# Six pairs of rounds convolved by VectorE instead of four, with each task's first product on ScalarE

## The chip, the core and the metric

The kernel runs on one core of one Trainium2 chip. The core has five engines, each with its own instruction queue: TensorE (PE in the profile, with its weight loads as PEld), VectorE (DVE), ScalarE (ACT), GpSimd (POOL) and SyncE (SP). An engine works through its queue in order, so an instruction that waits holds up everything behind it. Data move between DRAM and the on-chip memory SBUF by DMAs, which are issued from SP and POOL and share 16 DMA engines. TensorE writes to PSUM, from which ScalarE and VectorE take the results.

The metric is the time of one execution in microseconds (us). Less is better.

## What is computed

A causal convolution over seven tokens, whose taps are softmaxed per head of 24 channels, and then a feed-forward part without a bias (cut from the reference):

```
w = exp(weight - max); w = w / (sum(w) + 1e-09)           # 8 heads x 7 taps
x_pad = concatenate([zeros(B, 6, D), x], axis=1)          # B=8, S=3904, D=192
out[b, s, h*24+g] = sum_k w[h, k] * x_pad[b, s + k, h*24+g]
a = conv @ w1                                             # 31232 x 192 @ 192 x 1024
b = conv @ w2
h = a * b @ w3                                            # w3: 1024 x 1024
return h @ w_out                                          # w_out: 1024 x 192
```

The kernel multiplies w3 by w_out once, at the start (`w3_product`, into `W_sb`), so that each token costs two products with 1024 columns and one product back to 192.

## The kernel before

**Rounds.** The 31232 tokens are two streams of 15616 (NS = 2), worked side by side in the upper and lower 64 partitions. A round is 512 tokens of both streams (CH = 512); there are 31, and the last has 256. `first_product` (L471) forms a and b for a round in eight tiles of 128 columns: six matmuls into `pa`, six into `pb` (L486); ScalarE casts `pa` to `asb` (L493), and VectorE multiplies `asb` by `pb` into `abT` (L495). `second_product` (L505) takes one stream of a round: 32 matmuls into `ops` (L511), a copy to `osb` by ScalarE (L516), and a DMA to the output from SP (L521). PSUM is four buffers in rotation, each for one `pa`, `pb`, `ops` or `cps`.

**Phases.** After rounds 0 to 2, the loop at L672 goes through phases. Phase 0 has no first product; phase p has the first products of rounds 2p+1 and 2p+2. Each phase then has the second products of two earlier rounds, four calls numbered n = 0 to 3. Everything else is put between these by hand, in program order: that order is the order of each engine's queue.

**The convolution on TensorE.** `conv` (L300) multiplies windows of 32 tokens (26 of them new) by banded matrices, in small matmuls of 32x32 (`cps`, L318), which ScalarE and VectorE cast into `convo` (L327). Windows come in batches; `SIZES` (L49) gives their sizes after the first three of 20: 40, 40, 40, 80, 80, 80, 32. A batch of 40 or 32 from the fifth on is convolved in two units of 64 matmuls, one of 80 in four units of 32 matmuls; the dictionary `places` (L649) says after which second product of which phase a unit comes. `x_jobs` loads a batch from POOL (`xb`, L152), paced by a one-row copy that waits for an `abT` (L679). `store` writes `convo` to a DRAM scratch `rows` from SP (L349, L356), and `transposes` (L390) reads it back by DMA transposes, also from SP, into the ring `xT`, from which `first_product` takes its operand.

**The convolution on VectorE.** The rounds of the phases in `SIDE` = (4, 7, 10, 13) skip that path. For each such pair of rounds there are three tasks, one per 64 channels. A task casts its part of x to bf16 in DRAM by two DMAs from POOL (`rows_c`, L417), reads it back transposed by two DMA transposes from SP (`raw`, L427), and convolves in `side_conv` (L430): a first product (L437), then six passes of multiply and add over 128x1024 (L444), the last of them into `side`. Where a sequence starts inside the span, five of the six passes are cut in two and one element is zeroed. One task runs in each of the three phases before its pair is used, as a block between the first and second products of the phase; `convolve` (L660) gives both casts of a unit to ScalarE in such a phase, and else one of them to VectorE.

**Around the start.** `later_loads` (L614) queues on POOL the loads of w3, w_out, batches 3 to 5 and the two casts of the first task. At tile 4 of round 2 (L639) come the last part of `w3_product`, the last unit of batch 3, its store, and the transposes of rounds 3 and 4.

Of the kernel before, what the change touches and what calls it, by code (L numbers as in the profile page):

```python
# [16 lines left out]
def kernel(  # L17
# [10 lines left out]
    nc = tc.nc  # L28

    B, S, D = x.shape  # L30
    H, K = weight.shape
    G = D // H
# [22 lines left out]
    def phase_of(R):  # L55
        return (R - 1) // 2
# [13 lines left out]
    spans = [(0, t0), (t0, t0 + SIZES[4] * ST), (t0 + SIZES[4] * ST, (2 * SIDE[0] + 1) * CH)]  # L70
    for q, nxt in zip(SIDE, SIDE[1:] + (NR,)):
        spans.append(((2 * q + 3) * CH, min((2 * nxt + 1) * CH, TS)))
# [11 lines left out]
    const = ctx.enter_context(tc.tile_pool(name="const", bufs=1))  # L84
    stage = ctx.enter_context(tc.tile_pool(name="stage", bufs=2))
# [15 lines left out]
    rows_c = dram.tile([TS, NP, NS * Q], BF16, name="rows_c")  # L101
# [71 lines left out]
    for r in range(NS):  # L173
        p = group(r, 0).start
# [12 lines left out]
        out=diag, in_=diag, pattern=[[-1, 128 + 8]], compare_op=ALU.is_equal,  # L187
# [85 lines left out]
    p = group(1, 0).start  # L273
# [130 lines left out]
                              in_=taps_d[h:h + 1, :].to_broadcast([c1 - c, K]))  # L404
            c = c1

    raw_of, side_of = {}, {}

    def side_span(p):
        return (2 * p + 1) * CH, (2 * p + 3) * CH  # L410

    def side_cast(p, k):
# [10 lines left out]
    def side_transpose(p, k):  # L423
        t0, t1 = side_span(p)
        raw_of[p, k] = stage.tile([128, HALO + 2 * CH], BF16, tag="w3T", bufs=2, name="raw")
        for lo, hi in ((t0 - HALO, t0 + CH), (t0 + CH, t1)):
            nc.sync.dma_start_transpose(  # L427
                out=raw_of[p, k][:, HALO + lo - t0:HALO + hi - t0], in_=rows_c[lo:hi, k, :])

    def side_conv(p, k):  # L430
        t0, t1 = side_span(p)
        if p not in side_of:
            side_of[p] = stage.tile([128, NP, 2 * CH], BF16, tag="w3b0", bufs=1, name="side")
        raw = raw_of.pop((p, k))
        acc = stage.tile([128, 2 * CH], FP32, tag="w3b4", bufs=1, name="acc")
        starts = [z for z in range(0, TS, S) if t0 <= z < t1]
        nc.vector.tensor_scalar(  # L437
            out=acc, in0=raw[:, HALO - 1:HALO - 1 + t1 - t0], scalar1=wC[:, k, K - 2:K - 1],
            scalar2=None, op0=ALU.mult)
        for z in starts:  # L440
            nc.vector.memset(acc[:, z - t0:z - t0 + 1], 0.0)

        def add(out, lo, hi, d):
            nc.vector.scalar_tensor_tensor(  # L444
                out=out, in0=raw[:, HALO + lo - t0 - d:HALO + hi - t0 - d],
                scalar=wC[:, k, K - 1 - d:K - d], in1=acc[:, lo - t0:hi - t0],
                op0=ALU.mult, op1=ALU.add)

        for d in range(2, K):
            for lo, hi in zip([t0] + [z + d for z in starts], starts + [t1]):  # L450
                add(acc[:, lo - t0:hi - t0], lo, hi, d)
        add(side_of[p][:, k, :], t0, t1, 0)

    def operand(R, k, rs):
        if phase_of(R) in SIDE:
# [97 lines left out]
    def load_w3(j0, n, quarters=range(4)):  # L553
        if j0 not in w3b_of:
            t = stage.tile([128, 4 * n, GQ], BF16, tag=f"w3b{j0}", bufs=1, name="w3b")
            for j in range(j0, j0 + n, 2):
                w3b_of[j] = (t, 4 * (j - j0))
        t = w3b_of[j0][0]
        for i in quarters:
            nc.gpsimd.dma_start(  # L560
                out=t[C * i:C * i + C],
                in_=bass.AP(tensor=moe_w3.tensor, offset=j0 * 128 * DFF + i * GQ,
                            ap=[[DFF, C], [C * DFF, 4 * n], [1, GQ]]))
# [41 lines left out]
        swap_w(k, HC + 256, DFF, P)  # L605
    load_w3(0, 4, range(2, 4))

    def seq(*fs):
        def run():
            for f, *a in fs:  # L610
                f(*a)
        return run

    def later_loads():  # L614
        nc.gpsimd.tensor_scalar(out=taps, in0=taps, scalar1=total, scalar2=None, op0=ALU.mult)
        load_x(3)
        load_wo()
        load_w3(4, 2)
        load_w3(6, 2)
        load_x(4)  # L620
# [23 lines left out]
    phases = [()] + [(R, R + 1) for R in range(LAG + 1, NR, 2)]  # L644
    assert phases[-1][-1] == NR - 1
# [6 lines left out]
    tasks = {q - NP + k: (q, k) for q in SIDE for k in range(NP)}  # L652
    jobs = {p: side_cast(*tasks[p + 1]) for p in range(1, len(phases)) if p + 1 in tasks}
    for p, b, part in ((1, 6, 0), (2, 6, 1), (3, 7, 0), (4, 7, 1), (6, 8, 0), (7, 8, 1), (9, 9, 0)):
        jobs[p] = jobs.get(p, []) + x_jobs(b, part)
    points = ((0, 1), (0, 3), (0, 5), (0, 7), (1, 2), (1, 4))
    sent = [LAG + 3]
    due = []

    def convolve(p):  # L660
        b, h, n = units.pop(0)
        conv(b, h * G, n * G, (V, A) if p not in tasks else (A, A))
        if h + n == H:
            store(b)
            while sent[0] < len(conv_rounds) and \
                    min((conv_rounds[sent[0]] + 1) * CH, TS) <= spans[b - 3][1]:
                due.append(conv_rounds[sent[0]])
                sent[0] += 1
# [1 line left out]
    pace = const.tile([1, 2], BF16)  # L670
    done = 0
    for p, rounds in enumerate(phases):  # L672
        if p == 0:
            P(out=wC[Q:128], in_=wC[0:Q])
        todo = jobs.pop(p, [])

        def issue(R, ft, n):
            def run():
                P(out=pace, in_=abT_of[R][0:1, ft, 1, 0:2])  # L679
                for _ in range(min(n, len(todo))):  # L680
                    todo.pop(0)()
            return run

        each = -(-len(todo) // len(points))
        for j, R in enumerate(rounds):
            first_product(R, {ft: issue(R, ft, each) for a, ft in points if a == j and todo})
        assert not todo
        for b in {u[0] for u in units[:3]}:
            for xb, p0, w in zero_rows.pop(b, []):
                nc.gpsimd.memset(xb[p0:p0 + PAD, w, :], 0.0)  # L690
        if p + 1 in tasks:
            side_transpose(*tasks[p + 1])
        if p in tasks:
            side_conv(*tasks[p])
        last = NR if p == len(phases) - 1 else done + 2
        seconds = [(R, r) for R in range(done, last) for r in range(NS)]
        done = last
        for n, (R, r) in enumerate(seconds):
            (last_product if (R, r) == (NR - 1, NS - 1) else second_product)(R, r)
            if n in places.get(p, ()):  # L700
                convolve(p)
        for R in due[:2]:
            transposes(R)
        del due[:2]
# [31 lines left out]
```

## Time and profile before

| What | Value |
|---|---|
| median of three runs | 516.99 us (516.53 to 517.62) |
| the profiled execution | 516.74 us, of which the span of its instructions is 514.9 us |
| TensorE's granted clock | 0.999 |
| PE matmul busy | 510.1 us, 99% of the span |
| DVE busy | 418.2 us, 81% |
| ACT busy | 340.2 us, 66% |
| POOL busy | 90.3 us, 18% |
| mean of one `abT` multiplication (L495, DVE) | 1221 ns, 240 of them |
| mean of one `asb` cast (L493, ACT) | 1012 ns, 244 of them |
| mean of one `osb` copy (L516, ACT) | 799 ns, 60 of them at 128x768 |
| one pass over 128x1024 (L444, DVE) | 1285 ns |
| one first product over 128x1024 (L437, DVE) | 748 ns, 12 of them |
| `cps` matmuls (L318, PE) | 1088 |
| DMA packets moved for POOL's queue, for SP's queue | 17.44 MB, 42.73 MB |

Busy time is the time in which an engine has an instruction in work; it says how full an engine is, not whether anyone waits for it. Three other views say that. The chain of work that ended last is followed back from the last instruction, at each step to whatever released it; its pieces have a start and a length. The timeline lists instructions by start, merged where they follow each other closely, with the number of instructions after an x, and with the idle time ahead of them and its releaser in square brackets. The view of the DMA queues counts packets and bytes in a stretch of time.

### The profile page before, as it was taken

What the parts mean: (1) busy time and instruction counts of PE and PEld (TensorE: products, weight loads), DVE (VectorE), ACT (ScalarE), POOL (GpSimd) and SP (SyncE); (2) the same over time, 40 slices, a digit from 0 to 9 for tenths busy, and PEclk for the clock granted to TensorE, in tenths of its full rate; (3) what the DMA queues carried; (4) which work ended last, traced back from release to release, by engine and by line L of the source; (5) the groups of instructions that cost most, each with busy time, mean ns of one, the idle gap of its engine ahead of it and who ended that gap; (6) DMA issues with size and microseconds to landing.
All of it is one profiled execution on the core that took longest, in us unless ns stands there. A gap on an engine that the chain in (4) does not pass through costs nothing.

```text
span 514.9 us, 14364 instructions
## 1 busy us (share of the span) xinstructions
PE 510.1 (99%) x6148; PEld 334.5 (65%) x6148; DVE 418.2 (81%) x410; ACT 340.2 (66%) x392; POOL 90.3 (18%) x191
## 2 busy tenths in 40 slices
PE   9999999999999999999999999999999999999997
PEld 4446946758567585675856758567585675846787
DVE  7898389699796997979979899797997979977370
ACT  7786476674768737677576475767747657376562
POOL 9965021040220401002030010320101000000000
PEclk9999999999999999999999999999999999999999
DMA  9999599898575998039599872835949171210304
GB/s 141 150 166 185 123 163 203 166 146 153 71 96 138 184 153 160 23 124 82 105 150 179 187 72 80 106 45 144 155 115 144 23 190 27 75 51 1 123 1 155
DMA packets 149744, 61.19 MB, mean 119 GB/s; under 512 B 102708, under 2 KB 149680, under 8 KB 149680
## 3 DMA queue, kind: packets, MB, share of 16 engines
q1 hardware_dynamic: 88848, 42.73, 37.3%
q0 software_dynamic: 60672, 17.44, 35.0%
q8 instruction: 48, 0.79, 0.6%
q14 instruction: 16, 0.13, 0.1%
q10 hardware_dynamic: 160, 0.10, 0.1%
HBM read 35.16 MB, written 34.85 MB: 136 GB/s over the span
## 4 chain that ended last, share of the span: by engine, by line
PE 95%; POOL 3%; ACT 0%; issue 0%; DVE 0%; POOLq 0%
PE ops L511 32%; PE pa L486 30%; PE pb L486 30%; PE cps L318 2%; POOL ws L214 1%; PE wps L579 1%; POOL xb L152 1%; PE tps L365 0%; PE ops L532 0%; DVE abT L495 0%; POOL w3b L560 0%; POOL wn L220 0%; POOL wn L221 0%; POOL wn L223 0%; POOL wn L222 0%
## 5 line engine op out<-in xcount | busy, mean ns | idle before, releaser
L495 DVE TENSOR_TENSOR abT<-asb,pb 128x1024 bf16<-128x1024 bf16 x240 | 292.9, 1221 | 71.6 <-ACT asb L493 56.0
L493 ACT CAST asb<-pa 128x1024 bf16<-128x1024 f32 x244 | 247.0, 1012 | 63.3 <-PE pa L486 63.1
L486 PEld LDWEIGHTS <-wn 64*128 64x128 bf16 x1488 | 138.2, 94 | 85.1 <-issue 2.2
L486 PEld LDWEIGHTS <-ws 64*128 64x128 bf16 x1488 | 131.1, 94 | 71.3 <-POOL ws L214 1.1
L511 PE MATMUL ops<-W_sb,abT 128*128 128x192 bf16 x1936 | 165.5, 247 | 0.0
L511 PEld LDWEIGHTS <-abT 128*128 128x128 bf16 x1936 | 158.1, 98 | 8.5 <-issue 8.1
L486 PE MATMUL pb<-xT,wn 64*128 64x512 bf16 (+1 forms) x552 | 146.7, 372 | 0.0
L486 PE MATMUL pa<-xT,wn 64*128 64x512 bf16 (+1 forms) x552 | 145.8, 372 | 0.2
L486 PE MATMUL pa<-xT,ws 64*128 64x512 bf16 (+1 forms) x552 | 145.9, 372 | 0.0
L486 PE MATMUL pb<-xT,ws 64*128 64x512 bf16 (+1 forms) x552 | 144.7, 372 | 0.1
L516 ACT COPY osb<-ops 128x768 f32<-128x768 f32 (+1 forms) x61 | 48.4, 793 | 99.0 <-PE ops L511 99.0
L444 DVE SCALAR_TENSOR_TENSOR acc<-raw,wC,acc 128x1024 f32<-128x1024 bf16 (+10 forms) x90 | 78.7, 925 | 1.3
L679 POOL COPY pace<-abT 1x2 bf16<-1x2 bf16 x52 | 9.1, 174 | 282.7 <-DVE abT L495 282.7
L486 PE MATMUL pb<-side,wn 64*128 64x512 bf16 x192 | 52.0, 376 | 0.0
L486 PE MATMUL pa<-side,wn 64*128 64x512 bf16 x192 | 51.8, 376 | 0.0
L486 PE MATMUL pa<-side,ws 64*128 64x512 bf16 x192 | 51.8, 377 | 0.0
L486 PE MATMUL pb<-side,ws 64*128 64x512 bf16 x192 | 51.4, 376 | 0.0
L152 POOL DMA_DIRECT2D xb<-in_x_dram x64 | 40.8, 642 | 13.0 <-issue 6.3
L327 ACT CAST convo<-cps 128x640 bf16<-128x640 f32 (+4 forms) x70 | 39.1, 637 | 1.6 <-PE cps L318 1.5
L417 POOL DMA_DIRECT2D rows_c<-in_x_dram x24 | 18.6, 778 | 6.9 <-issue 6.9
L444 DVE SCALAR_TENSOR_TENSOR side<-raw,wC,acc 128x1024 bf16<-128x1024 bf16 x12 | 15.4, 1285 | 0.4
L318 PE MATMUL cps<-xb,Aband 32*32 32x120 bf16 (+2 forms) x1088 | 13.3, 233 | 0.0
(65 smaller groups left out, 101.4 us busy)
## 6 DMA issues: line engine op xcount, KB each, us to landing
out_dram<-osb SPq DMA_DIRECT2D x58, 384.0 KB
xb<-in_x_dram POOLq DMA_DIRECT2D x28, 240.0 KB, 6.4
rows_c<-in_x_dram POOLq DMA_DIRECT2D x24, 130.0 KB, 4.8
rows<-convo SPq DMA_DIRECT2D x9, 240.0 KB
xb<-in_x_dram POOLq DMA_DIRECT2D x8, 228.0 KB, 10.4
rows<-convo SPq DMA_DIRECT2D x9, 150.0 KB
xb<-in_x_dram POOLq DMA_DIRECT2D x8, 168.0 KB, 4.4
rows<-convo SPq DMA_DIRECT2D x9, 120.0 KB
```

The lines of the kernel that those rows point to most:

```text
L152: nc.gpsimd.dma_start(out=tiles[js[0]][0][group(r, e), s:s + w, :], in_=bass.AP(tensor=x.tensor, offset=(r * TS + t - PAD) * D, ap=[[D, C] ...
L214: f(out=wsw[k][Q * h:Q * h + Q, lo:hi], in_=wn[k][Q - Q * h:2 * Q - Q * h, lo:hi])
L318: nc.tensor.matmul(o.rearrange("p (w g) -> p w g", g=wd)[:, :, c - c0:c1 - c0], Aband[group(r, e), h, :], xb[group(r, e), s:s + m, c:c1], ...
L327: f(out=convo[:, e::E, k, :, lo:lo + c] .rearrange("p w r g -> p r w g"), in_=src[:, :, :, o:o + c])
L417: nc.gpsimd.dma_start(out=rows_c[t0 - HALO:t1, k, r * Q:r * Q + Q], in_=x_rows[r * TS + t0 - HALO:r * TS + t1, k * Q:k * Q + Q])
L444: nc.vector.scalar_tensor_tensor(out=out, in0=raw[:, HALO + lo - t0 - d:HALO + hi - t0 - d], scalar=wC[:, k, K - 1 - d:K - d], in1=acc[:, ...
L486: nc.tensor.matmul(p[:, r, f * N:f * N + N], w_of(i, k, r)[rs, ft * 128:(ft + 1) * 128], operand(R, k, rs), start=(k == 0), stop=(k == NP ...
L493: nc.scalar.copy(out=asb[:, :, 0:per * N], in_=pa[:, :, 0:per * N])
L495: nc.vector.tensor_tensor(out=ab[:, f0, :, 0:N], in0=asb[:, :, 0:N], in1=pb[:, :, 0:N], op=ALU.mult)
L511: nc.tensor.matmul(ops[:, g // 2, (g % 2) * D:(g % 2) * D + D], ab[:, jt, r, g * 128:(g + 1) * 128], W_sb[:, jt, :], start=(jt == 0), stop ...
L516: nc.scalar.copy(out=osb.rearrange("p (a g) d -> p a (g d)", g=2), in_=ops[:, 0:ng // 2, 0:2 * D])
L679: P(out=pace, in_=abT_of[R][0:1, ft, 1, 0:2])
```

## The change

- `SIDE` becomes (3, 7, 8, 11, 12, 14): six pairs of rounds, eighteen tasks. The last pair has 768 tokens, the others 1024. The batches after the first three of 20 become 40, 40, 80, 40, 80, 40.
- The spans of the batches follow from `SIDE` by a loop in place of a list.
- A task's first product is an ACTIVATE with a scale on ScalarE (`side_first`); the six passes stay on VectorE (`side_sums`) but are dealt out one by one: eight to a phase that has units in `places`, seven to one that has none, beginning in phase 0. A task can begin in one phase and end in the next. Its first product is put ahead of second product n on ScalarE, with n from how far its phase is filled.
- There are five `raw` buffers, two `acc` and two `side`, in place of two, one and one. Both casts of a unit go to ScalarE in every phase that has passes.
- The casts of a task's x are queued a phase ahead of its start, and more of them where the phase has few loads. The first two tasks' casts come ahead of batch 4 in `later_loads`, their transposes on SP ahead of the store of batch 3 at tile 4 of round 2, and the copy of half the taps, `wC`, goes from GpSimd to ScalarE.

```diff
-    SIDE = (4, 7, 10, 13)
-    SIZES = [20, 20, 20, 40, 40, 40, 80, 80, 80, 32]
+    SIDE = (3, 7, 8, 11, 12, 14)
+    SIZES = [20, 20, 20, 40, 40, 80, 40, 80, 40]
...
+    def side_tiles():
+        for _ in range(2):
+            t = stage.tile([128, 2 * RAW], BF16, tag="w3T", bufs=2, name="raw")
+            raw_of.extend((t[:, 0:RAW], t[:, RAW:2 * RAW]))
+        for tag in ("w3b4", "w3b6"):
+            acc_of.append(stage.tile([128, 2 * CH], FP32, tag=tag, bufs=1, name="acc"))
+        a = stage.tile([128, NP * 2 * CH + RAW], BF16, tag="w3b0", bufs=1, name="side")
+        raw_of.append(a[:, NP * 2 * CH:])
+        b = const.tile([128, NP * 2 * CH], BF16, name="side")
...
+    def side_first(i):
+        p, k = tasks[i]
         t0, t1 = side_span(p)
-        nc.vector.tensor_scalar(
-            out=acc, in0=raw[:, HALO - 1:HALO - 1 + t1 - t0], scalar1=wC[:, k, K - 2:K - 1],
-            scalar2=None, op0=ALU.mult)
+        nc.scalar.activation(
+            out=acc_of[i % 2][:, 0:t1 - t0], in_=raw_of[i % 5][:, HALO - 1:HALO - 1 + t1 - t0],
+            func=ACT.Copy, scale=wC[:, k, K - 2:K - 1])
...
+    places = {0: (0, 1), 1: (2,), 2: (0, 1, 2), 3: (0,), 4: (0,), 6: (0, 2), 7: (0, 2),
+              10: (0,), 11: (0,)}
+    starts, chain, room, p = {}, {}, 0, -1
+    for i, (q, k) in enumerate(tasks):
+        for cost, f in side_sums(i):
+            while room < cost:
+                p += 1
+                room = 8 if p in places else 7
+                at, free = 0, 0
+                starts.setdefault(p, [])
+            if not chain or chain[max(chain)][-1][0] != i:
+                starts[p].append(i)
+                n = min(2 * NS - 1, -int(-free * 0.48))
+                chain.setdefault(p, []).append((i, n, lambda i=i: side_first(i)))
+            room, at = room - cost, at + cost
+            chain.setdefault(p, []).append((i, None, f))
+        free = at
...
+        for i in starts[0]:
+            for f in side_cast(i):
+                f()
         load_x(4)
-        for f in side_cast(SIDE[0], 0):
+        for i in starts[1]:
+            for f in side_cast(i):
+                f()
+        for f in x_jobs(5, 0):
             f()
-        load_x(5)
...
+               (A, wC[Q:128], wC[0:Q]), (side_tiles,), *[(side_transpose, i) for i in starts[0]],
                (store, 3), (transposes, 3), (transposes, 4))})
...
-    places = {0: (0, 1), 1: (0, 2), 2: (2,), 3: (0, 1, 2), 5: (0, 2), 6: (0, 2),
-              8: (0, 2), 9: (0, 2), 10: (0,), 11: (0,)}
...
-        conv(b, h * G, n * G, (V, A) if p not in tasks else (A, A))
+        conv(b, h * G, n * G, (V, A) if p not in chain else (A, A))
...
-        if p == 0:
-            P(out=wC[Q:128], in_=wC[0:Q])
...
-        if p + 1 in tasks:
-            side_transpose(*tasks[p + 1])
-        if p in tasks:
-            side_conv(*tasks[p])
+        for i in starts.get(p + 1, ()):
+            side_transpose(i)
+        state = set()
...
         for n, (R, r) in enumerate(seconds):
+            side_steps(p, n, state)
```

`side_steps` emits, ahead of second product n, each first product that is due, and then the passes in their order up to the next first product that is not yet out. By the changed program's lists of instructions, the first products fall as follows: ahead of n = 0 in phases 0, 2, 3, 5, 6, 9, 10 and 12 (one each), and a second one in phases 0, 3 and 12 ahead of n = 2 and in phases 6 and 10 ahead of n = 3; the only one of phases 1, 4 and 8 ahead of n = 1, of phases 7 and 11 ahead of n = 2. TensorE has 960 `cps` matmuls in place of 1088. In phase 6 the second first product stands on ScalarE behind the four casts of the unit placed at n = 2 and ahead of the last `osb` copy.

More of the change, by code (lines that the diff above doesn't have):

```diff
@@ L69 @@
     t0 = (LAG + 3) * CH
-    spans = [(0, t0), (t0, t0 + SIZES[4] * ST), (t0 + SIZES[4] * ST, (2 * SIDE[0] + 1) * CH)]
-    for q, nxt in zip(SIDE, SIDE[1:] + (NR,)):
-        spans.append(((2 * q + 3) * CH, min((2 * nxt + 1) * CH, TS)))
+    spans = [(0, t0)]
+    for R in range(LAG + 3, NR):
+        if phase_of(R) in SIDE:
+            continue
+        if R % 2 and (phase_of(R) - 1 in SIDE + (LAG - 1,) or
+                      (spans[-1][1] - spans[-1][0]) >= 4 * CH):
+            spans.append((R * CH, R * CH))
+        spans[-1] = (spans[-1][0], min((R + 1) * CH, TS))
     wins = []
@@ L405, in load_taps, with side_cast @@
             c = c1
-    raw_of, side_of = {}, {}
     def side_span(p):
-        return (2 * p + 1) * CH, (2 * p + 3) * CH
-    def side_cast(p, k):
+        return (2 * p + 1) * CH, min((2 * p + 3) * CH, TS)
+    tasks = [(q, k) for q in SIDE for k in range(NP)]
+    side_of, acc_of, raw_of = {}, [], []
+    RAW = HALO + 2 * CH
+    def side_tiles():
[7 more added lines that the diff above has]
+        b = const.tile([128, NP * 2 * CH], BF16, name="side")
+        for i, q in enumerate(SIDE):
+            side_of[q] = (a if i % 2 == 0 else b)[:, 0:NP * 2 * CH].rearrange(
+                "p (k t) -> p k t", k=NP)
+    def side_cast(i):
+        p, k = tasks[i]
         t0, t1 = side_span(p)
@@ L421, in side_cast, with side_transpose @@
         return [job(r) for r in range(NS)]
-    def side_transpose(p, k):
+    def side_transpose(i):
+        p, k = tasks[i]
         t0, t1 = side_span(p)
-        raw_of[p, k] = stage.tile([128, HALO + 2 * CH], BF16, tag="w3T", bufs=2, name="raw")
         for lo, hi in ((t0 - HALO, t0 + CH), (t0 + CH, t1)):
             nc.sync.dma_start_transpose(
-                out=raw_of[p, k][:, HALO + lo - t0:HALO + hi - t0], in_=rows_c[lo:hi, k, :])
-    def side_conv(p, k):
+                out=raw_of[i % 5][:, HALO + lo - t0:HALO + hi - t0], in_=rows_c[lo:hi, k, :])
@@ L431, in side_conv @@
+    def side_first(i):
+        p, k = tasks[i]
         t0, t1 = side_span(p)
[L432 to L435, printed above, removed]
-        starts = [z for z in range(0, TS, S) if t0 <= z < t1]
-        nc.vector.tensor_scalar(
-            out=acc, in0=raw[:, HALO - 1:HALO - 1 + t1 - t0], scalar1=wC[:, k, K - 2:K - 1],
-            scalar2=None, op0=ALU.mult)
@@ L440, in side_conv @@
[L440 to L451, printed above, removed]
@@ L452, in side_conv, with side_sums, job, run @@
-        add(side_of[p][:, k, :], t0, t1, 0)
+        nc.scalar.activation(
+            out=acc_of[i % 2][:, 0:t1 - t0], in_=raw_of[i % 5][:, HALO - 1:HALO - 1 + t1 - t0],
+            func=ACT.Copy, scale=wC[:, k, K - 2:K - 1])
+    def side_sums(i):
+        p, k = tasks[i]
+        t0, t1 = side_span(p)
+        starts = [z for z in range(0, TS, S) if t0 <= z < t1]
+        def job(d, last):
+            def run():
+                raw, acc = raw_of[i % 5], acc_of[i % 2]
+                if d == 2:
+                    for z in starts:
+                        nc.vector.memset(acc[:, z - t0:z - t0 + 1], 0.0)
+                for lo, hi in [(t0, t1)] if last else \
+                        zip([t0] + [z + d for z in starts], starts + [t1]):
+                    a = acc[:, lo - t0:hi - t0]
+                    nc.vector.scalar_tensor_tensor(
+                        out=side_of[p][:, k, 0:t1 - t0] if last else a,
+                        in0=raw[:, HALO + lo - t0 - d:HALO + hi - t0 - d],
+                        scalar=wC[:, k, K - 1 - d:K - d], in1=a, op0=ALU.mult, op1=ALU.add)
+            return run
+        size = (t1 - t0) / (2 * CH)
+        return [(size, job(d, d == 0)) for d in list(range(2, K)) + [0]]
@@ L606, with side_steps @@
     load_w3(0, 4, range(2, 4))
+    phases = [()] + [(R, R + 1) for R in range(LAG + 1, NR, 2)]
+    assert phases[-1][-1] == NR - 1
+    places = {0: (0, 1), 1: (2,), 2: (0, 1, 2), 3: (0,), 4: (0,), 6: (0, 2), 7: (0, 2),
[12 more added lines that the diff above has]
+                chain.setdefault(p, []).append((i, n, lambda i=i: side_first(i)))
+            assert p < q
+            room, at = room - cost, at + cost
+            chain.setdefault(p, []).append((i, None, f))
+        free = at
+    for p in starts:
+        for i in starts[p]:
+            assert i < 5 or p < 2 or max(v for v in chain if chain[v][0][0] <= i - 5) <= p - 2
+    def side_steps(p, n, state):
+        items = chain.get(p, [])
+        for v, (i, at, f) in enumerate(items):
+            if at is not None and at <= n and v not in state:
+                state.add(v)
+                f()
+        for v, (i, at, f) in enumerate(items):
+            if at is None and v not in state:
+                state.add(v)
+                f()
+            elif v not in state:
+                break
     def seq(*fs):
@@ L648 @@
              for h in range(0, H, n)]
-    places = {0: (0, 1), 1: (0, 2), 2: (2,), 3: (0, 1, 2), 5: (0, 2), 6: (0, 2),
-              8: (0, 2), 9: (0, 2), 10: (0,), 11: (0,)}
     assert sum(map(len, places.values())) == len(units)
[L652 to L655, printed above, removed]
+    jobs = {p: [] for p in range(1, len(phases))}
+    for p, b, part in ((1, 5, 1), (2, 6, 0), (4, 7, 0), (5, 7, 1), (8, 8, 0)):
+        jobs[p] += x_jobs(b, part)
+    casts = [(p - 1, f) for p in starts if p > 1 for i in starts[p] for f in side_cast(i)]
+    for p in jobs:
+        due_now = sum(d <= p for d, _ in casts)
+        ahead = max(due_now, min(len(casts), 6 - len(jobs[p])))
+        jobs[p] = ([f for _, f in casts[:due_now]] + jobs[p] +
+                   [f for _, f in casts[due_now:ahead]])
+        del casts[:ahead]
     points = ((0, 1), (0, 3), (0, 5), (0, 7), (1, 2), (1, 4))
@@ L701 @@
                 convolve(p)
+        assert len(state) == len(chain.get(p, ()))
         for R in due[:2]:
```

6 lines of the change are left out of this document (3 added, 3 removed).

## The prediction, on record before the changed kernel ran

> **What bounds the kernel.** I read the busy time first, then the chain of work that ended last.
>
> ```profile
> PE 510.1 (99%) x6148; PEld 334.5 (65%) x6148; DVE 418.2 (81%) x410; ACT 340.2 (66%) x392; POOL 90.3 (18%) x191
> ...
> PE 95%; POOL 3%; ACT 0%; issue 0%; DVE 0%; POOLq 0%
> ```
>
> TensorE is busy for 99% of the span at a granted clock of 0.999, and the chain runs over it but for the start. So time goes only where TensorE gets fewer instructions, and comes only where TensorE is made to wait. Next the chain's pieces in order of time (start, length):
>
> ```profile
> 52.25 2.75 PE ops L511 x32
> 55.00 0.66 PE cps L318 x64
> ...
> 85.27 2.75 PE ops L511 x32
> ...
> 118.29 8.03 PE ops L511 x96
> ...
> 150.25 2.75 PE ops L511 x32
> ...
> 183.12 10.67 PE ops L511 x128
> ...
> 214.62 2.75 PE ops L511 x32
> ```
>
> These are the starts of the second products of phases 0 to 5. From 183.12 (phase 4, no unit) to 214.62 is 31.50 us: a phase without convolution. The others exceed it by their units, and nothing else: phase 0, 33.02 with two units of 64 `cps` matmuls, so 0.76 us each; phase 2, 31.96 with one unit of 32, 0.46; phase 3, 32.87 with three, 0.457 each. Hence no phase has a hidden stall of TensorE, and a unit costs its matmuls (0.66 above) and some 0.1 of changeover.
>
> **Fewer matmuls.** Before: batches 4 and 5 have two units of 64 each, 6 to 8 four of 32, 9 two of 64 smaller ones; the last cost 0.79 and 0.74 us (phases 10 and 11: second products start at 375.78, 408.07 and 440.31, less 31.50). The sum is 4 x 0.76 + 12 x 0.457 + 1.53 = 10.05 us. After: three batches of 40 and two of 80, 6 x 0.76 + 8 x 0.457 = 8.22. The gain is **1.83 us**, for 128 `cps` matmuls of 1088. All of it lies on the bound engine. Loads of `x`, stores and ring transposes of a pair of rounds go too; they were hidden.
>
> **VectorE.** The timeline of VectorE over phases 5 and 6:
>
> ```profile
> 228.05 20.65 DVE L495 TENSOR_TENSOR abT<-asb,pb 128x1024 bf16<-128x1024 bf16 x16 [3.05 <-ACT asb L493]
> 248.61 0.75 DVE L437 TENSOR_SCALAR acc<-raw,wC 128x1024 f32<-128x1024 bf16 x1
> 249.40 0.35 DVE L444 SCALAR_TENSOR_TENSOR acc<-raw,wC,acc 128x128 f32<-128x128 bf16 x1
> 249.42 0.06 DVE L441 MEMSET acc<- 128x1 f32 x1
> 249.66 6.42 DVE L444 SCALAR_TENSOR_TENSOR acc<-raw,wC,acc 128x894 f32<-128x894 bf16 x9
> 256.12 1.28 DVE L444 SCALAR_TENSOR_TENSOR side<-raw,wC,acc 128x1024 bf16<-128x1024 bf16 x1
> 260.46 2.52 DVE L495 TENSOR_TENSOR abT<-asb,pb 128x1024 bf16<-128x1024 bf16 x2 [3.06 <-ACT asb L493]
> ```
>
> The multiplications are paced by TensorE (20.65 for sixteen); behind the block VectorE idles 3.06 us. Between the last multiplication and the next phase's first lie 31.50 - 20.65 = 10.85 us, plus the phase's units. A whole pass takes 1.313 us from start to start (phase 1: 87.63 to 95.51 for six), a cut one 1.346 (249.40 to 256.12 for five). Seven passes: 9.2 us in 10.85. Eight cut ones, at worst (phases 0, 1, 2, 3): 10.75 us in 12.37, 11.31, 12.22 and 11.61; later 10.5 in 11.6 or more. So each phase's sums fit, the tightest (phase 1) with 0.55 us left, and VectorE costs **nothing**. Its cover is this gap. If it is gone, TensorE stands for the overrun less 0.28 us (next part), at the third tile's `pb`, whose PSUM buffer the first multiplication frees.
>
> **ScalarE's first product.** No row has it. Nearest: `asb`, 128x1024 from PSUM, 1012 ns; from SBUF, `xb` casts of 32x1152 in 1151 ns and 32x576 in 667, a slope of 0.84 ns and 0.18 fixed, so 1.04 us for 1024. I take 1.05; the ends are 0.75 (VectorE's L437) and 1.35. Most stand where ScalarE idles 0.75 us or more afterwards, or where the next `osb` is late by under 0.5, which its rotating buffer absorbs. One does not: phase 6, behind four casts. Its model is phase 5 of before, with the same units:
>
> ```profile
> 223.14 0.80 ACT L516 COPY osb<-ops 128x768 f32<-128x768 f32 x1 [1.84 <-PE ops L511]
> 223.84 1.95 ACT L327 CAST convo<-cps 128x320 bf16<-128x320 f32 x4
> 226.24 0.80 ACT L516 COPY osb<-ops 128x768 f32<-128x768 f32 x1 [0.45 <-PE ops L511]
> 227.00 1.01 ACT L493 CAST asb<-pa 128x1024 bf16<-128x1024 f32 x1
> ```
>
> The casts end at 225.79. With 1.05 us behind them `osb` starts at 226.84, 0.60 late, and so does everything queued behind: `asb`, then the multiplication that follows it, ending 229.87 instead of 229.27. TensorE wants that buffer at 226.21 + 0.75 + 4 x 0.65 = 229.55: slack was 0.28, the stall is **0.3 us** (0 to 0.65 at the ends). Lateness dies out within a few tiles, ScalarE needing 1.01 of each 1.296 us. `wC`'s copy (some 0.2 us on ScalarE instead of GpSimd, 64x21) falls ahead of round 2's sixth `asb` and costs 0 to 0.1: nothing.
>
> **DMAs.** Casts 24 to 36; transposes stay at 84 (24 to 36 of `raw`, 60 to 48 of `xT`). SP and POOL have slack in every phase, except at the start. SP there, before:
>
> ```profile
> 49.63 4.64 SPq L356 DMA_DIRECT2D rows<-convo  x8
> 54.32 0.48 SPq L349 DMA_DIRECT2D rows<-convo  x1
> 54.90 9.68 SPq L390 DMA_TRANSPOSE xT<-rows  x6
> ```
>
> Four transposes of `raw` now stand ahead of batch 3's store. They can start when the second half of `w3_product` begins to free its buffers, about 46.3 (its matmuls run 44.85 to 47.6), and take 1.25 us each (median), so the store starts at 51.4, 1.8 us later than 49.63. Round 3 needs its third transpose at 64.87; before, that was issued by 59.7 and its packets ended at 60.7. Slack is some 4 us, less what a completion takes to be seen, which no row shows; so the delay is hidden: **nothing**. Its cover is the four second products of phase 0. With `raw`'s slowest row (2.26 each) the store starts at 55.4, 5.8 us late, and TensorE waits 2.
>
> POOL's queue is full until 52. The other loads queued there are as large as before (batch 5's 960 KB are now half a batch of 80), so four casts come on top. Between 46.0 and 46.6 casts moved 497 packets, 0.10 MB; a cast is 1040 packets, 130 KB, so 0.8 to 1.3 us, four 3 to 5. Batch 4 then lands not by 46 but by 51; TensorE needs it at 55.00: nothing. But the backlog runs to 57 and meets the store. Between 51.4 and 52.0 the hardware queue had 58.8% and the software queue 51.7% of the engines' time (overlap counted), about half each. The Trainium skill, DMA: Bandwidth & Descriptors, SWDGE vs HWDGE vs iDMA, says that each DMA engine takes turns between the two; the trace agrees here. The same page, Specifications, says that descriptors under 512 B are read, modified and written, so the casts' 128 B rows should cost twice their bytes, as an estimate 6 us for four; the trace disagrees, moving 0.10 MB of casts in the time of 0.11 MB of `xb` (49.0 to 49.6). By that rule the backlog would reach 58, and the sum would stay.
>
> **Sum.** 516.74 - 1.83 + 0.3 = 515.2 for an execution like the profiled one, which was 0.25 below the median of 516.99; against the median, **515.5**.
>
> **Rivals.**
> - *The sums fit but ScalarE's order costs more.* Phase 6 at 0.65 and phases 0 to 3 at some 0.1 each (their margins are thin): 515.9 to 516.2. For: phase 1's 0.55 us. Against: lateness under 0.28 is free. Chance 0.10.
> - *Start partly late.* The store shares the DMA engines with the backlog (its 3.8 us of moving become 5.5 or more) and `raw` takes 1.6 us (as the six `xT` at 54.90 did: 9.68/6). Then round 3's transposes land 4.5 to 6.5 us late, TensorE waits 0.5 to 2.5: 516.0 to 518.0, likeliest 516.6, no change. For: DMA engines saturated to 52 already. Against: 4 us of slack. Chance 0.20.
> - *Slower: SP's queue at the start.* One mechanism: `raw` transposes ahead of the store at 2.26 us (9.0 us), then store and transposes at half share (3.5 us more): 5.8 + 3.5 = 9.3 late, TensorE waits 5.3, 520.8. It decides from 6.5 us of lateness, 4 of slack and 2.5 from 515.5 to 518.0. First products of tasks 0 and 1 would then also hold ScalarE's `osb` behind them. For: `raw` took 2.26 and 1.72 at 114.56 under load. Against: the usual 1.25 to 1.5. Chance 0.13.
> - *No gain*, since the matmuls were hidden: TensorE at 99% and phases that differ by just their units speak against it: 517.0, chance 0.02.
>
> **Chances.** Forecast 0.55 (515.0 to 515.9, faster). A measurement can tell 0.2%, 1.0 us, from no change. Faster: 0.55 + half the first rival + a fifth of the second = 0.64; slower: 0.13; same: 0.23. The range reaches from 514.8 (gain 1.83 less spread of the runs, 0.4) to 517.6, which leaves out the third rival and the end of the second.
>
> **What would show it.** Right: phases of 31.50 us plus 0.457 or 0.76 per unit; first products of 1.05 us; only phase 6 longer, by 0.3; the first matmul of round 3 at 64.4. Wrong: a gap of TensorE ahead of round 3, idle time of TensorE's loads released by `xT`; VectorE's last pass ending after `asb` is ready; first products near 1.35 us.

## The result and the profile after

The change made the kernel slower. The median of 17 executions is 518.57 us (517.15 to 521.57) against 516.87 us for the kernel before (17 executions, 516.53 to 518.19): a ratio of 1.0037, with a 95% interval of 1.0024 to 1.005. The profiled execution took 520.86 us, with a span of 519.2. Seven of the 17 executions, the profiled one among them, have a mean granted clock of 0.997 and took 518.57 to 521.57 us; the other ten have 1.000 and took 517.15 to 518.90. The amounts below are read from the profiled execution, which is 2.3 us above the median, so the median execution loses less than they say.

Busy time and chain on the page of the profile after:

```profile
PE 510.7 (98%) x6020; PEld 336.4 (65%) x6020; DVE 446.5 (86%) x430; ACT 353.3 (68%) x403; POOL 87.4 (17%) x178
...
PE 92%; DMA 3%; ACT 2%; DVE 1%; SPq 1%; issue 0%
```

TensorE has 128 matmuls fewer, as said, but 0.6 us more busy time: some of its work ran slower. And the chain now runs over DMAs and SP's queue for a few per cent, where before TensorE had 95%.

The chain's pieces give the starts of the second products, phase by phase, to be laid beside those of before:

```profile
91.47 8.03 PE ops L537 x96
...
123.43 2.75 PE ops L537 x32
...
220.81 10.67 PE ops L537 x128
252.31 2.75 PE ops L537 x32
...
285.09 2.75 PE ops L537 x32
```

The first line is phase 1, and the others are phases 2, 5, 6 and 7. Phase 1's second products start at 91.47 instead of 85.27, 6.20 us late. From there on the kernel is the faster one. The last second products start here, before and after the change:

```profile
498.18 11.99 PE ops L511 x144
```

```profile
502.87 11.99 PE ops L537 x144
```

From phase 1's second products to the last ones it takes 411.40 us (91.47 to 502.87), where before took 412.91 (85.27 to 498.18): 1.51 us gained. Behind the start of the last ones it is 0.4 us quicker too (16.33 us to the end of the span, was 16.72), which need not be the change: s5 below takes 17.07 there. So from phase 1's second products on the change did what it was forecast to do, and **the whole loss lies between 46 and 91 us**.

There, SP's timeline (start, length, count):

```profile
46.36 5.85 SPq L448 DMA_TRANSPOSE raw<-rows_c  x4
52.33 8.54 SPq L361 DMA_DIRECT2D rows<-convo  x8
61.06 0.31 SPq L354 DMA_DIRECT2D rows<-convo  x1
63.39 7.08 SPq L395 DMA_TRANSPOSE xT<-rows  x5
```

Against before, the first `xT` transpose is issued 8.5 us late (63.39, was 54.90), in three parts. The store starts at 52.33 instead of 49.63: 2.7. It takes 9.04 us to its end instead of 5.17: 3.9; the view of waits puts 3.7 us of it down to `raw`, which had to land first. Then the transpose waits 2.0 us for the store to land, where it waited 0.1: 1.9. The view of waits (us in total, times, longest):

```profile
SPq L361 <- DMA raw<-rows_c: 3.7, 3, 1.4
SPq L395 <- DMA rows<-convo: 2.0, 2, 1.3
```

The chain says the same, and what follows from it:

```profile
53.84 9.53 DMA rows<-convo
63.39 1.13 SPq L395
...
66.59 2.69 DMA xT<-rows
```

The third transpose is issued at 66.59, and its data release TensorE at 69.3. TensorE's timeline shows round 3 standing there:

```profile
67.28 0.37 PE L512 MATMUL pa<-xT,wn 64*128 64x512 bf16 x1 [0.87 <-ACT osb L542]
...
69.32 0.37 PE L512 MATMUL pa<-xT,wn 64*128 64x512 bf16 x1 [0.92 <-DMA xT<-rows]
```

Before, that third pair of matmuls came at 64.82 in the same view, so the data are 4.50 us late. The remaining 1.70 us of the 6.20 come next. By windows (TensorE, its weight loads, VectorE, ScalarE, GpSimd, then the granted clock):

```profile
68.00:70.00 2.00, 1.07 (x8) 0.50 (x9) 1.20 (x2) 0.25 (x1) 0.00 (x0) 0.92 0.56 127
70.00:72.00 2.00, 2.00 (x14) 0.80 (x10) 1.00 (x1) 0.76 (x1) 0.00 (x0) 0.50 0.33 74
72.00:74.00 2.00, 2.00 (x16) 0.94 (x14) 0.77 (x2) 1.01 (x1) 0.00 (x0) 0.72 0.59 126
```

Behind the gap the clock falls to 0.50. At full speed the three windows would have been worth 2 x (0.08 + 0.50 + 0.28) = 1.72 us more, as much as 3.4 us at half speed. The Trainium skill, TensorE: Matmul & The Clock Gate, What's actually happening, says that the clock halves after an idle window of about 3.4 us, that windows run free of the program, and that as long a busy stretch brings it back. The length of the slow stretch, 3.4 us, agrees here; TensorE had not idled for a whole window, though, but had 0.80 us of matmuls in the 2.9 us from 66.4 to 69.3.

### The profile page after: what moved, and what is told of

Its sections match the earlier page's. It is cut to its first block, busy times and chain, and to the rows that moved or that the text cites. A ratio compares the mean times of both kernels' runs of the same rounds, so it can differ in the third digit from the quotient of the medians.

```text
span 519.2 us, 14128 instructions
## 1 busy us (share of the span) xinstructions
PE 510.7 (98%) x6020; PEld 336.4 (65%) x6020; DVE 446.5 (86%) x430; ACT 353.3 (68%) x403; POOL 87.4 (17%) x178
## 3 DMA queue, kind: packets, MB, share of 16 engines
q0 software_dynamic: 66912, 17.07, 36.7%
## 4 chain that ended last, share of the span: by engine, by line
PE 92%; DMA 3%; ACT 2%; DVE 1%; SPq 1%; issue 0%
PE pa L512 30%; PE pb L512 30%; PE ops L537 28%; DMA rows<-convo 2%; PE cps L323 2%; PE wps L605 1%; ACT asb L519 1%; ACT convo L332 1%; DVE abT L521 1%; PE warm L233 1%; SPq L395 1%; DMA xT<-rows 1%; DMA out_dram<-osb 0%; PE ops L558 0%; PE tps L385 0%
## 5 line engine op out<-in xcount | busy, mean ns | idle before, releaser
L512 PE MATMUL pa<-xT,wn 64*128 64x512 bf16 x456 | 124.1, 378 | 2.0 <-DMA xT<-rows 0.9
L512 PE MATMUL pb<-xT,wn 64*128 64x512 bf16 x456 | 125.2, 379 | 0.0
L512 PE MATMUL pa<-xT,ws 64*128 64x512 bf16 x456 | 124.2, 379 | 0.3 <-DMA xT<-rows 0.3
L512 PE MATMUL pb<-xT,ws 64*128 64x512 bf16 x456 | 123.0, 379 | 0.0
L472 DVE SCALAR_TENSOR_TENSOR acc<-raw,wC,acc 128x1024 f32<-128x1024 bf16 (+3 forms) x100 | 93.9, 973 | 1.3
L512 PE MATMUL pb<-side,wn 64*128 64x512 bf16 (+1 forms) x288 | 75.0, 368 | 0.2 <-DVE abT L521 0.2
L512 PE MATMUL pa<-side,wn 64*128 64x512 bf16 (+1 forms) x288 | 74.5, 368 | 0.0
L512 PE MATMUL pa<-side,ws 64*128 64x512 bf16 (+1 forms) x288 | 74.4, 368 | 0.0
L512 PE MATMUL pb<-side,ws 64*128 64x512 bf16 (+1 forms) x288 | 73.7, 368 | 0.0
L332 ACT CAST convo<-cps 128x640 bf16<-128x640 f32 (+2 forms) x62 | 34.1, 633 | 1.8 <-PE cps L323 1.7
```

The source lines that it names most:

```text
L332: f(out=convo[:, e::E, k, :, lo:lo + c] .rearrange("p w r g -> p r w g"), in_=src[:, :, :, o:o + c])
L472: nc.vector.scalar_tensor_tensor(out=side_of[p][:, k, 0:t1 - t0] if last else a, in0=raw[:, HALO + lo - t0 - d:HALO + hi - t0 - d], scalar ...
L512: nc.tensor.matmul(p[:, r, f * N:f * N + N], w_of(i, k, r)[rs, ft * 128:(ft + 1) * 128], operand(R, k, rs), start=(k == 0), stop=(k == NP ...
```

## The experiments

After this look four causes were in question. **A**: GpSimd's backlog, its queue of casts and loads of `x`, delays the store and round 3's transposes. **B**: the order on SP does, four `raw` transposes ahead of the store. A and B can act together. **C**: the phases are too full, for VectorE or ScalarE; the phases above, each as long as its units say, speak against it. And the order on ScalarE: its first product at 57.24 waited 4.53 us for `raw`, and `osb` and the casts behind it held TensorE (idle before `cps` 0.46 and 0.69 us, before `ops` 0.21). All times are medians, and each is compared with runs of the kernel before on the same chip (516.82 to 516.86 us).

**s1_load_later: a smaller backlog.** The load of batch 5's first half goes from the start to phase 1.

```diff
-        for f in x_jobs(5, 0):
-            f()
...
-    for p, b, part in ((1, 5, 1), (2, 6, 0), (4, 7, 0), (5, 7, 1), (8, 8, 0)):
+    for p, b, part in ((1, 5, 0), (1, 5, 1), (2, 6, 0), (4, 7, 0), (5, 7, 1), (8, 8, 0)):
```

> The changed kernel with one edit: the first half of batch 5 (960 KB, four DMAs of GpSimd) is loaded in phase 1 instead of at the start. Theory A, that GpSimd's backlog of DMAs at the start holds up batch 3's store and round 3's transposes: the backlog ends some 5 us sooner (about 55 instead of 60), round 3 starts by 66.5 instead of 69.3, and the time falls to 515.5 to 516.5. Theory B, that it is the order on SyncE (four transposes of raw ahead of the store): the store still starts at 52, round 3 still waits for its transposes, 517.5 to 518.5. Theory C, that the time is lost in the phases (VectorE and ScalarE too full): no change, 518.5.

It took 522.65 us, ratio 1.0108 (1.0086 to 1.0129). The start did improve: the first `xT` transpose came at 59.00 instead of 63.39, and round 3's third pair was 1.1 us late instead of 4.50. The store starts as late as in the changed kernel (52.09), but no longer waits for `raw` and is issued by 58.88. But a new wait took its place, by the chain:

```profile
84.24 0.08 issue
84.32 0.18 POOL pace L747
84.50 0.29 issue
84.79 0.51 POOL xb L157
85.30 13.91 DMA xb<-in_x_dram
```

Issued at 84.79 behind its pace, the half batch lands at 99.2, and TensorE waits 3.8 us for it before phase 1's `cps`, so the time that A forecast did not come. The backlog is part of the cause, B is left for the other part, and this load can't be moved there.

**s2_first_at_1: ScalarE freed.** The first task's first product goes behind one second product of phase 0.

```diff
-                n = min(2 * NS - 1, -int(-free * 0.48))
+                n = 1 if i == 0 else min(2 * NS - 1, -int(-free * 0.48))
```

> The changed kernel with one edit: ScalarE's first product of task 0 stands ahead of the second of phase 0's second products instead of the first, so that its wait for raw (4.5 us in the trace) no longer holds the first osb copy. If this wait decides (its share of TensorE's idle time was 1.4 us ahead of the second cps, 0.9 ahead of round 3): 516.5 to 517. If round 3's transposes decide, TensorE only waits longer there: no change, 518 to 519, with the time that the cps no longer lose appearing ahead of round 3.

It took 520.45 us, 1.0062 (1.0043 to 1.0082) (the profiled execution 520.86, like that of the changed kernel). TensorE no longer stands before `cps`; it stands longer for `xT` (0.69 + 0.68 + 2.58 us), and phase 1's second products start at 91.45, where they did. So the order on ScalarE is not the cause: its wait is real, but round 3's data come last anyway. The time is above the 518 to 519 forecast for that case.

**s3_raw_behind_xT: another order on SP.** The first task's transposes go behind those of round 3, phase 0 gets two passes instead of eight, the others eight.

```diff
-                room = 8 if p in places else 7
+                room = 8 if p else 2
...
-                n = min(2 * NS - 1, -int(-free * 0.48))
+                n = 3 if i == 0 else min(2 * NS - 1, -int(-free * 0.48))
...
-               (A, wC[Q:128], wC[0:Q]), (side_tiles,), *[(side_transpose, i) for i in starts[0]],
-               (store, 3), (transposes, 3), (transposes, 4))})
+               (A, wC[Q:128], wC[0:Q]), (side_tiles,), (store, 3), (transposes, 3),
+               *[(side_transpose, i) for i in starts[0]], (transposes, 4))})
```

> The changed kernel with the transposes of raw behind those of round 3 on SyncE. Since raw then lands late, phase 0 has two passes of VectorE and its first product stands ahead of the last second product; every later phase has eight. Only task 0 (two transposes) is due there, and two casts fewer are queued at the start. Theory B (order on SyncE): the store starts at 49.6 as before the change, round 3 starts at 64.5 to 65, 515 to 516. Theory A (backlog): store and transposes move at half rate until 57 to 60, round 3 starts at 66 to 68, 517 to 518.5.

It took 518.23 us, 1.0023 (1.0014 to 1.0033). The store starts at 49.93 and the `xT` transposes at 56.30, and round 3 waits for nothing: with nothing ahead of the store on SP, it is not late. (Two casts fewer stand at the start, too; s7 below has four more than before, and no wait either.) But `raw` now lands late. The first product starts at 65.98 after 2.85 us of waiting, VectorE's passes run from 67.34 to 70.07, ahead of phase 1's first multiplication, and phase 1's second products start at 88.59, still 3.3 us late. The loss moved to ScalarE and VectorE: TensorE waits 0.88 us for an `osb` behind the first product and 0.74 us for a multiplication.

**s4_both: one task at the start, the half batch later.** Phase 0 gets four passes, so only one task (two transposes) stands ahead of the store; the half batch is moved as in s1; and where a unit stands at n = 2, no first product goes behind it.

```diff
-                room = 8 if p in places else 7
+                room = 8 if p else 4
...
-                n = min(2 * NS - 1, -int(-free * 0.48))
+                n = 1 if i == 0 else min(2 if 2 in places.get(p, ()) else 3, -int(-free * 0.48))
```

> Three edits together: batch 5's first half loaded in phase 1; only task 0 begun in phase 0, with four passes (its two transposes ahead of the store), eight passes in each later phase; no first product behind the casts of a unit ahead of the last osb copy. By theories A and B alike the start is then as before the change (round 3 at 64.4 to 65), and every phase is 31.50 us plus its units: 516.9 - 1.8 = 515.0 to 515.4. Theory C: 517 or more, with phases longer than 31.50 plus units, those of eight passes without a unit above all.

It took 523.61 us, 1.0127 (1.0103 to 1.0151). The start is clean (store at 49.91, `xT` at 55.11, no wait of round 3), and phase 6 takes 32.42 us, so the stall of 0.36 there is gone. Nearly all of the loss is the half batch, which again lands too late (85.69 to 100.56): 5.3 us of waiting, behind which the clock is 0.50 from 100 to 104.

**s5_one_task: the same with the half batch loaded at the start again.**

> The kernel of s4_both with batch 5's first half loaded at the start again, as in the changed kernel. What is left of its edits: only task 0 begins in phase 0 (two transposes of raw ahead of the store and two casts fewer at the start), and no first product in ScalarE's way in phase 6. Theory B (the transposes ahead of the store): the store starts at 49.9, round 3 waits for nothing, and phase 1 has its batch: 515.0 to 515.5. Theory A (GpSimd's backlog): the two casts left on top are some 2.5 us of DMA, the store shares with them, round 3 waits 0.5 to 2 us: 515.5 to 517.

It took **515.87 us** (515.23 to 517.30), ratio 0.9977 (0.9967 to 0.9988): faster than the kernel before, and the best of all versions. Its SP timeline, and from its chain the third transpose:

```profile
46.22 2.60 SPq L448 DMA_TRANSPOSE raw<-rows_c  x2
49.54 5.95 SPq L361 DMA_DIRECT2D rows<-convo  x8
...
57.73 8.71 SPq L395 DMA_TRANSPOSE xT<-rows  x6
```

```profile
60.85 4.32 DMA xT<-rows
```

With two transposes ahead instead of four, the store starts when it did before. The third transpose releases TensorE at 65.17; the third pair of round 3 comes 0.4 us later than before, 0.3 of it a wait, and phase 1's second products start at 85.68. By B alone there was to be no wait and at most 515.5 us; the wait of 0.3 us and the 515.87 lie between the two forecasts or within A's, so the backlog still counts a little. From there to the last ones it is 411.05 us, 1.86 less than before: the forecast gain of 1.83, with no stall in phase 6. Of that 0.99 us is left between the medians: 0.4 us is lost ahead of phase 1's second products, and some 0.35 us behind the last ones (17.07 us to the end of the span, was 16.72).

**s6_paced_loads: and the loads behind held back.** As s5, with the second task's casts and the half batch held until round 2's last multiplication.

```diff
-        for i in starts[1]:
-            for f in side_cast(i):
-                f()
-        for f in x_jobs(5, 0):
-            f()
...
+    P(out=first_pace, in_=abT_of[2][0:1, 7, 1, 0:2])
+    for i in starts[1]:
+        for f in side_cast(i):
+            f()
+    for f in x_jobs(5, 0):
+        f()
```

> As s5_one_task, but task 1's casts and batch 5's first half are held on GpSimd until round 2's last abT (about 54 us), so that the store has the DMA engines to itself. Theory A: round 3 starts on time (64.4 to 64.6), 515.0 to 515.3, and better than s5_one_task by the wait seen there. Rival: the loads held back now meet the transposes of round 3 (55 to 60) and land later, so that either round 3 or phase 1's batch waits: 515.5 to 518.

It took 517.44 us, 1.0032 (1.0001 to 1.0062): the rival that its forecast names. The store meets less traffic (first `xT` transpose at 55.17), but the held loads meet the transposes: the third, issued at 57.90, takes 9.15 us to release TensorE, which waits 1.7 us for `xT`. Two of the ten executions took 522.75 and 523.70 us.

**s7, s8 and s10: the parts alone, on the kernel before.** s7_casts_alone adds four casts that nothing reads ahead of batch 4's load. s8_casts_and_raw adds to that their four transposes, ahead of the store, into a buffer that nothing reads. s10_two_raw_alone adds no work, but puts the first task's own two casts ahead of batch 4 and its two transposes ahead of the store.

```diff
+        for k in range(2):
+            for f in side_cast(3, k):
+                f()
         load_x(4)
...
-               (store, 3), (transposes, 3), (transposes, 4))})
+               (early_raw,), (store, 3), (transposes, 3), (transposes, 4))})
```

The first half is s7, both are s8. s10:

```diff
-        load_x(4)
         for f in side_cast(SIDE[0], 0):
             f()
+        load_x(4)
...
-               (store, 3), (transposes, 3), (transposes, 4))})
+               (side_transpose, SIDE[0], 0), (store, 3), (transposes, 3), (transposes, 4))})
...
-        if p + 1 in tasks:
+        if p + 1 in tasks and p:
```

> The kernel before with four more casts (of data that nothing uses) ahead of batch 4's load on GpSimd: the DMA load of the changed start alone. Theory A: some 4 to 5 us of backlog more, store and transposes of round 3 at half rate to 57, round 3 waits 0 to 2 us: 517 to 519. Theory B: no change, 516.9.

> As s7_casts_alone, with four DMA transposes of those casts ahead of batch 3's store on SyncE, into a buffer that nothing reads: the whole of the changed start without its sums, so that ScalarE waits for nothing. If order and backlog together make the loss: the store at 52, round 3 late by 3 to 5 us, 520 to 523 (the clock falling after the gap). If ScalarE's wait for raw made it: 517 or less.

> The kernel before with its own first task's two casts ahead of batch 4's load and its two transposes of raw ahead of batch 3's store: the order on SyncE with two transposes and no DMA more. Estimated from s5_one_task, where two transposes ahead cost 0.4 us at the start: 516.9 to 517.4. If any transposes ahead of the store cost as the four of s8_casts_and_raw did (5.2 us for four): 519.5.

s7 took 517.01 us, 1.0011 (0.9996 to 1.0025), s10 516.98, 1.001 (0.9994 to 1.0026): no change that can be told. s8 took **522.23**, 1.0104 (1.0067 to 1.0141). SP's timeline of s8:

```profile
46.62 8.73 SPq L634 DMA_TRANSPOSE early<-rows_c  x4
55.46 5.73 SPq L356 DMA_DIRECT2D rows<-convo  x8
...
62.27 8.73 SPq L390 DMA_TRANSPOSE xT<-rows  x6
```

and of s10:

```profile
46.44 3.43 SPq L427 DMA_TRANSPOSE raw<-rows_c  x2
49.98 5.59 SPq L356 DMA_DIRECT2D rows<-convo  x8
...
56.76 9.17 SPq L390 DMA_TRANSPOSE xT<-rows  x6
```

s8 has none of the new sums, and nothing on ScalarE waits for its transposes, yet it loses nearly as much at the start as the changed kernel did: TensorE waits 1.82, 0.27 and 0.90 us for `xT`, the clock falls to 0.50, and phase 1's second products start at 90.70, against 91.47. It isn't a copy in every detail. Its second pair of transposes waited 3.2 us for the last added cast, which landed at 51.03, and so the store itself starts late; in the changed kernel the store starts earlier and is slow. The casts alone cost no time, and neither do two transposes alone; four transposes together with the casts cost 5.4 us. But both parts are only hidden: they put off the first `xT` transpose from 54.90 to 57.16 (s7) and to 56.76 (s10), 2.3 and 1.9 us, and s8 puts it off by 7.4. Four transposes without the casts were not run.

**s9_pair_4: nothing ahead of the store.** The first pair is phase 4's, so the sums begin in phase 1 and still 960 `cps` matmuls are left; the price is nine passes in phases 1 and 3, and eight elsewhere.

```diff
-    SIDE = (3, 7, 8, 11, 12, 14)
-    SIZES = [20, 20, 20, 40, 40, 80, 40, 80, 40]
+    SIDE = (4, 7, 8, 11, 12, 14)
+    SIZES = [20, 20, 20, 40, 40, 40, 80, 80, 40]
...
-                room = 8 if p in places else 7
+                room = {0: 0, 1: 9, 3: 9}.get(p, 8)
...
```

Spans, `places` and the loads of `x` follow from the new sizes, and first products keep clear of a unit's last casts, as in s4.

> Six pairs as in the changed kernel, but (4, 7, 8, 11, 12, 14): the first task begins in phase 1, so that no transpose of raw and no first product of a task stands at the start; the batches of 40 and 80 are the same in number (960 cps matmuls), the passes are nine in phases 1 and 3, eight elsewhere, and no first product stands behind a unit's casts ahead of the last osb copy. GpSimd has two casts more at the start than before the change. If the loss was the start alone: every phase 31.50 us plus its units, round 3 at 64.4, 516.86 - 1.83 = 515.0 (514.8 to 515.3). If fuller phases cost anything: phases 1 and 3 longer than 33.02 and 32.87, up to 516.5.

It took 516.19 us, 0.9987 (0.9978 to 0.9996). That is faster than before, but by less than half of the full gain. Phase 0's second products start 0.8 us late; 0.5 of it is a wait for the first `x` load (issued at 1.5 us), which the edit doesn't touch. Phases 1, 3 and 11 exceed 31.50 us and their units by 0.06, 0.06 and 0.23 us (in the last, the chain runs over VectorE's passes). And some 0.4 us lie outside of the profile: the time exceeds the span by 2.0 to 2.2 us in all eleven executions, against 1.7 to 1.8 in the changed kernel and in s5; what that is, no view shows.

## Why the prediction was wrong

- **What bounds the kernel, and fewer matmuls: right.** A gain of 1.83 us was forecast; 1.51 + 0.36 (phase 6) = 1.87 was measured, and 1.86 in s5.
- **VectorE: right.** The passes cost nothing in the changed kernel: phases without units take 31.49 to 31.50 us, and as much in s4 with eight passes. Nine in phases 1 and 3 of s9 cost 0.06 us each, and eight in phase 11 of s3 and s9 cost 0.23.
- **ScalarE's first product: right.** It takes 1151 ns in the median (forecast 1050) and, behind the start, stalls only phase 6, by 0.36 us (forecast 0.3). ScalarE's timeline of phase 6 shows the model's order:

```profile
261.53 1.96 ACT L332 CAST convo<-cps 128x320 bf16<-128x320 f32 x4
263.33 1.19 ACT L454 ACTIVATE acc<-side,wC 128x1024 f32<-128x1024 bf16 x1
264.38 0.83 ACT L542 COPY osb<-ops 128x768 f32<-128x768 f32 x1
```

- **DMAs at the start: the step that failed.** It said: "Slack is some 4 us, less what a completion takes to be seen, which no row shows; so the delay is hidden: **nothing**." Both sides were wrong. Of the two the delay decides: 1.8 us would still have been hidden by the slack of 2.4, and 8.5 us exceeds even 4.
  - The slack is about 2.4 us. The end of the packets was taken for the time at which TensorE gets the data. By the chains of s1, s2 and s5 the third transpose releases TensorE 4.3 to 4.4 us after its issue begins. The `xT` transposes may start at 57.16 (s7) without a wait, and at 57.73 (s5) TensorE waits 0.3; before, they started at 54.90. What "no row shows" was then left out of the sum instead of being bounded.
  - The delay is 8.5 us, where the step had 1.8. The issue time was the smaller part of it: the four `raw` took 5.85 us to issue, against some 5.0 in the sum. The rest is data that don't move. The DMA queues of the changed kernel from 46 to 50 us (packets, MB, share of the engines' time with overlap counted):

```profile
q0 software_dynamic: 2859, 0.70, 183.1%
```

  SP's queue (q1) has no line: after the first `raw` transpose was issued at 46.36 it moved nothing until 50.5, while GpSimd's queue filled the engines. From 51 to 52 both moved:

```profile
q0 software_dynamic: 318, 0.10, 86.6%
q1 hardware_dynamic: 294, 0.08, 56.3%
```

  That is nearly packet for packet, but less than half of the time for SP's queue. The prediction took half and half of the time from a stretch in which the store was already moving. The Trainium skill, DMA: Bandwidth & Descriptors, Queues, rings and completion order, says that a DMA engine takes turns between the queues that have work, packet by packet. The trace agrees from 51 to 52, as the profile counts packets; the four microseconds before don't show it. That the transposes had nothing to move by then is unlikely: in s4 and s6, with less queued on GpSimd, the first packets of the first `raw` transpose moved 1.3 us after its issue (47.9 after 46.59, and 47.6 after 46.29).
  - The store's issues then waited for `raw` to land (3.7 us), a wait that the prediction didn't have.
- **The rivals.** The third, SP's queue at the start, is what happened. It gave 9.3 us of lateness and 520.8 us; 8.5 us and 520.86 us were measured in the profiled execution, but the median is 518.57. Part of that is chance: its transposes were to be slow at 2.26 us each (they took 1.29 in the median, and the store was slow), and the fallen clock, 1.7 us, was in no rival. It was given 0.13, because 4 us of slack stood against it.

**What stays open.** Why ten of 17 executions show no drop of the clock, and about 518.1 us. Taking the drop's 1.7 us from 520.86 leaves 519.2, so the gap must be shorter in them too; no such execution was traced. Why no packet of SP's queue moved from 46.4 to 50.5. And why the store's issues wait for `raw`, of which the store reads nothing: they do in the changed kernel, s2 and s5, and not in s1, s4, s6 and s8.

## What to carry to other kernels

When DMAs are put ahead of others in a queue, count until the data release the engine, not until the packets end, and take from traces under the same load what the traffic ahead does to both; slack of a few microseconds at a loaded start is soon gone. Parts that cost no time alone (four casts; two transposes) may each have used up slack, and together with two transposes more they cost 5 us here: look at how late each makes the critical DMA, not only at the time. Where a change gains a little in each phase and loses once at the start, start it later or with less: one task instead of two ahead of the store kept the gain of the phases (1.86 us), and 0.99 of it in the median (515.87 us).

## What the runs showed of the hardware

- A gap of 2.9 us with 0.80 us of matmuls in it was followed by a granted clock of 0.50 for 2 us and below 1 in each window from 68 to 74, a loss of 1.7 us; s2 and s8 show the same (0.50 from 70 to 72). In s5, with a wait of 0.3 us, and in s6, with 1.7 us in two pieces, the clock stayed at 1.00 there.
- The third DMA transpose of `xT` released TensorE 4.3 to 4.4 us after its issue began in three runs, 2.7 in two, and 9.15 with half a batch and two casts beside it (s6).
- The first packet of a `raw` transpose moved 1.3 us after its issue in s4 and s6, and 4.2 us after it in the changed kernel and s5, where GpSimd's queue filled the engines (in the changed kernel 183.1% of their time from 46 to 50, overlap counted). From 51 to 52, with both queues moving, it was nearly packet for packet: 318 against 294 there, and 281 against 279 in s5; from 52 to 54 it was 744 against 424 in the changed kernel.
